# First expert layer in two halves of slots, v shift on VectorE, weight loads spread between scatters

## The chip, the cores and the metric

The kernel runs on one core of a Trainium2 chip (trn2). The metric is the device time of one execution in microseconds (us). A run is one execution, and a result below is the median of several. "Span" is the time from the first to the last instruction in the trace of one profiled execution; here time is the span plus about 2 us.

On three of the five occasions on which the kernel before was timed beside others it took 246 to 247 us, on the other two 262 to 263 us. I call these **fast chips** and **slow chip(s)**; only runs of one call share a chip. Chips 6, 1 and 12 were fast and chip 15 slow (the first call's chip is not on record). Each was timed in one call only, so a property of a chip cannot be told from a state that it was in.

## The reference, cut to what matters

```python
# q, k, v: (4, 8, 768, 64); heads 0, 2, 6 causal ("retrieval"), the other five: 4 sink keys and a window of 64
scores = q @ k.transpose(0, 1, 3, 2) / sqrt(64)          # masked per head
a = softmax(scores);  attn = a @ v
x = attn.transpose(0, 2, 1, 3).reshape(3072, 512)         # one row per token
for e in range(8):                                        # mixture of 8 experts
    mask = domain_id == e                                 # 3072 tokens, random expert each
    out[mask] = relu(x[mask] @ w1[e]) @ w2[e]             # w1: 512x1024, w2: 1024x512
```

Each expert gets about 384 tokens. The kernel gives it 448 slots (`CAP`), scatters each token's row into its slot in DRAM, and reads the slots back expert by expert.

## The kernel before, in the parts that the change touches

Attention goes batch by batch. Within a batch, short rounds of TensorE score products are mixed with older output products. The rows of batch b-1 are scattered in the middle of batch b. GpSimd issues all these scatters and all weight loads, in program order.

```python
    for b in range(B):
        ...
        vshift(b)                                   # 4 copies on GpSimd
        run_round([s_str_pair(b, 0, 0), ...], r0 + ...)
        run_round([s_str_pair(b, 1, 0), ...], r1 + t_units(b, 3))
        ...
        run_round([s_str_one(b, 2), s_sinks(b)], r2)
        if b:
            for t in range(NSO):                    # NSO = 6 blocks of 128 tokens
                scatter_x(b - 1, t)
        run_round([s_retr_pair(b, 3, 0), ...], [a_str_unit(b, 0)])
        if b + 2 < B:
            load_qk(b + 2, False); load_v(b + 2)
        if 0 < b < 3:
            load_w(wA, b - 1)                       # w1 and w2 of one expert, 2 MB
        ...
    for f in carry[0] + carry[1]:                   # last attention outputs
        f()
    for t in range(NSO):
        scatter_x(B - 1, t)
    load_w(wA, 2)
    ...
    load_x(0); load_x(1)                            # wait for every scatter; rows of 1 KB
    warm(16, "moe")                                 # junk matmuls
    x_transpose(0)
    load_w(wB, 3)
    for e in range(E):
        layer1(e)                                   # 32 matmuls of 448 columns
        if e + 1 < E: x_transpose(e + 1)            # 16 transposes, 3 VectorE copies
        if e + 2 < E: load_x(e + 2)
        layer2(e)                                   # 24 matmuls of 512 columns, scatter of the result
        if e + 4 < E: load_w(wB, e + 4)
```

`vshift` builds a copy of v in which odd 64-token blocks sit half a tile lower, so that the window of a streaming head lies in one tile.

The softmax here doesn't subtract the row's maximum and nothing guards it: scores larger than these inputs give would overflow.

## Time and profile before

| | time, median of 3 | lowest to highest | profiled execution |
|---|---|---|---|
| kernel before | 261.46 us | 261.29 to 263.63 | 245.93 us, span 244.1 us |

The profiled execution is some 16 us shorter than the timed ones.

Busy time by stretch of the trace (for each engine: busy us and number of instructions, then the granted TensorE clock as a share of full speed, the share of the DMA engines as the view gives it, which can pass 1, and GB/s), kernel before. PE is TensorE, PEld its weight loads, DVE VectorE, ACT ScalarE, POOL GpSimd, SP SyncE:

```profile
core 0: us, PE busy (x) PEld busy (x) DVE busy (x) ACT busy (x) POOL busy (x), PEclk, DMA share, GB/s
...
90.00:105.00 15.00, 11.81 (x249) 8.11 (x240) 9.70 (x25) 12.74 (x20) 8.84 (x15) 1.00 0.72 152
...
105.00:120.00 15.00, 3.87 (x28) 1.72 (x26) 1.10 (x3) 0.00 (x0) 9.69 (x16) 0.79 0.41 94
120.00:135.00 15.00, 8.89 (x47) 4.84 (x48) 1.30 (x3) 2.75 (x3) 0.00 (x0) 0.65 1.15 234
150.00:180.00 30.00, 30.00 (x178) 14.92 (x176) 8.66 (x15) 7.34 (x8) 12.63 (x21) 1.00 1.14 240
```

TensorE (PE) does 3.87 us of work in the 15 us from 105 on, and is busy without a gap from 150 to 180. The first row and the last are two stages, attention and experts; the hole is between them. What TensorE waits for there, from its list of waits (waited for: us in total, times, longest us):

```profile
PE tpx_0_2291 L767 <- DMA xe_2267<-x_slots: 16.4, 1, 16.4
```

`tpx` are the transposes of an expert's slots, `xe` the slots loaded; further below, `xT` are the transposed slots, `h` and `o` the products of the first and second layer, and `ob` the output copies. The loads can only start when the last scatter, issued 107.0 to 114.4 us, is done.

Three engines in batch 0 and later, kernel before. From GpSimd's timeline (start us, us, engine line op, [idle before <- releaser]), the shift of batch 0:

```profile
26.20 1.50 POOL L521 COPY vsh_123<-ve_145 64x1584 f16<-64x1584 f16 x1
27.74 1.28 POOL L522 COPY vsh_123<-ve_145 64x1320 f16<-64x1320 f16 x1
29.07 0.51 POOL L521 COPY vsh_123<-ve_145 64x396 f16<-64x396 f16 x1
29.64 0.46 POOL L522 COPY vsh_123<-ve_145 64x330 f16<-64x330 f16 x1
```

From TensorE's timeline, the product that waits for it:

```profile
29.63 0.21 PE L478 MATMUL avs_0_441<-vsh_123,eS_0_1_321 128*64 128x65 f16 x1 [4.70 <-POOL vsh_123 L521]
```

And from VectorE's timeline, the same small multiply with and without a GpSimd copy under way (the copy's line, from GpSimd's timeline, stands last):

```profile
86.88 0.17 DVE L224 TENSOR_TENSOR kbd<-kT_1_1731,ct 128x8 f16<-128x8 f16 x1
...
88.79 0.82 DVE L224 TENSOR_TENSOR kbd<-kT_2_1772,ct 128x8 f16<-128x8 f16 x1
...
88.09 1.50 POOL L521 COPY vsh_124<-ve_987 64x1584 f16<-64x1584 f16 x1
```

The multiply ends at 89.61 us, the copy at 89.59. The other such meeting in this trace is alike: the multiply took 0.97 us (65.74 to 66.71) and ended 0.02 us after the copy (65.19 to 66.69).

### The profile page before, as it was taken

How to read it: one execution, taken by the hardware profiler on the slowest of the kernel's cores; microseconds unless marked ns; L12 is line 12 of the kernel's file. 1: busy time of each engine (PE TensorE's matmuls, PEld its weight loads, DVE VectorE, ACT ScalarE, POOL GpSimd, SP SyncE). 2: the span in 40 equal slices, each digit the busy share in tenths (PEclk: the TensorE clock that was granted, in tenths of full speed). 3: DMA queues.
4: the chain of work that ended last, by engine and by line, in shares of the span. 5: the costliest groups of instructions: out<-in, count | busy, mean ns of one | idle time of the engine just before them, and what ended most of it. 6: DMA issues, size and time to landing. Idle time of an engine off the chain costs nothing. (4 is left out here: it accounts for less than half of the span.)

```text
span 244.1 us, 5013 instructions
## 1 busy us (share of the span) xinstructions
PE 187.0 (77%) x2077; PEld 108.3 (44%) x2077; DVE 98.0 (40%) x232; ACT 96.6 (40%) x133; POOL 109.6 (45%) x165
## 2 busy tenths in 40 slices
PE   6374269879748986880039999999999999999930
PEld 2262136756634773540024555454545454455410
DVE  0577093687995587420020313223240404141220
ACT  2157047789765798910003232141405050323200
POOL 8741956048937476538300161616154313313240
PEclk9657555799995799998557999999999999999985
DMA  6999999903999999302999999999999991203120
GB/s 121 221 212 175 196 173 201 126 34 103 169 178 200 227 256 214 104 26 103 180 242 229 220 262 197 248 245 221 276 231 278 226 266 64 82 3 121 44 83 1
DMA packets 55026, 41.26 MB, mean 169 GB/s; under 512 B 27196, under 2 KB 48596, under 8 KB 54998
## 3 DMA queue, kind: packets, MB, share of 16 engines
q0 software_dynamic: 49392, 35.67, 87.6%
q1 hardware_dynamic: 5606, 5.22, 7.9%
q8 instruction: 17, 0.28, 0.4%
q14 instruction: 11, 0.09, 0.1%
HBM read 56.62 MB, written 11.53 MB: 279 GB/s over the span
## 5 line engine op out<-in xcount | busy, mean ns | idle before, releaser
L767 PE MATMUL tpx_0_2291<-ct,xe_2267 128*128 128x128 f16 x8 | 1.0, 311 | 16.4 <-DMA xe_2267<-x_slots 16.4
L503 POOL DMA_INDIRECT x_slots<-xb_252,dest_i x6 | 6.4, 1062 | 12.1 <-ACT qT_3_868 L217 11.0
L794 ACT ACTIVATE hT_2316<-h_0_0_2317 128x896 f16<-128x896 f32 x1 | 0.9, 917 | 26.1 <-PE h_0_0_2317 L787 26.1
L801 POOL DMA_INDIRECT out_dram<-ob_2391,idx_i x1 | 1.1, 1053 | 21.3 <-DVE ob_2391 L800 21.3
L503 POOL DMA_INDIRECT x_slots<-xb_736,dest_i x6 | 6.4, 1067 | 6.1 <-DVE xb_736 L425 5.0
L767 PEld LDWEIGHTS <-xe_2267 128*128 128x128 f16 (+1 forms) x16 | 1.4, 137 | 17.1 <-DMA xe_2267<-x_slots 16.9
L503 POOL DMA_INDIRECT x_slots<-xb_1775,dest_i x6 | 5.9, 982 | 6.9 <-issue 6.9
L771 DVE COPY xT_2290<-tpx_0_2291 128x1024 f16<-128x1024 f16 x1 | 0.7, 690 | 20.2 <-PE tpx_0_2291 L767 20.2
L503 POOL DMA_INDIRECT x_slots<-xb_1286,dest_i x6 | 6.1, 1008 | 2.3 <-ACT eS_3_1926 L371 1.2
L258 PEld LDWEIGHTS <-ct 128*128 128x128 f16 x72 | 4.9, 111 | 4.8 <-issue 4.8
L787 PEld LDWEIGHTS <-w_0_990 128*128 128x128 f16 x32 | 3.4, 109 | 4.7 <-issue 2.5
L527 PEld LDWEIGHTS <-zt 128*128 128x128 f16 x26 | 2.7, 111 | 5.1 <-issue 2.0
L527 PE MATMUL warm_start<-zt 128*128 128x512 f16 x10 | 3.8, 556 | 1.3 <-DVE zt L669 1.3
L186 DVE COPY vs_sink<-vpat 128x1320 f16<-128x1320 f16 x1 | 2.2, 2232 | 6.3 <-DMA vpat<-vpat_c 6.3
L478 PEld LDWEIGHTS <-eS_0_1_321 128*64 128x64 f16 x24 | 1.9, 150 | 6.5 <-issue 6.5
L191 POOL DMA_DIRECT2D vs_sink<-in_v_dram x5 | 2.9, 577 | 4.0 <-DMA k_136<-in_k_dram 2.1
L180 POOL DMA_DIRECT2D ve_158<-in_v_dram x1 | 2.2, 2216 | 5.1 <-DMA ve_145<-in_v_dram 5.1
L801 POOL DMA_INDIRECT out_dram<-ob_3139,idx_i x1 | 1.0, 980 | 7.8 <-DVE ob_3139 L800 7.8
L787 PEld LDWEIGHTS <-w_7_2818 128*128 128x128 f16 x32 | 3.1, 98 | 3.0
L787 PEld LDWEIGHTS <-w_5_2565 128*128 128x128 f16 x32 | 3.1, 98 | 3.0
L787 PEld LDWEIGHTS <-w_1_1533 128*128 128x128 f16 x32 | 3.1, 98 | 3.0
L787 PEld LDWEIGHTS <-w_3_2312 128*128 128x128 f16 x32 | 3.1, 98 | 3.0
(887 smaller groups left out, 630.7 us busy)
## 6 DMA issues: line engine op xcount, KB each, us to landing
x_slots<-zt SPq DMA_DIRECT2D x8, 128.0 KB, 7.1
w_0_990<-in_moe_w_dram POOLq DMA_DIRECT2D x1, 1024.0 KB, 17.6
w_0_992<-in_moe_w_dram POOLq DMA_DIRECT2D x1, 1024.0 KB
w_1_1533<-in_moe_w_dram POOLq DMA_DIRECT2D x1, 1024.0 KB, 11.5
w_1_1535<-in_moe_w_dram POOLq DMA_DIRECT2D x1, 1024.0 KB
w_2_2241<-in_moe_w_dram POOLq DMA_DIRECT2D x1, 1024.0 KB, 9.1
w_2_2243<-in_moe_w_dram POOLq DMA_DIRECT2D x1, 1024.0 KB, 15.7
w_3_2312<-in_moe_w_dram POOLq DMA_DIRECT2D x1, 1024.0 KB, 21.4
```

The source lines that it names most:

```text
L180: nc.gpsimd.dma_start(out=ves[b][:, :, :, 0:D].rearrange("p h t d -> p (h t) d"), in_=v[b].rearrange("h (t p) d -> p (h t) d", p=P),)
L186: nc.vector.tensor_copy(out=vs_sink[:], in_=vpat[:].unsqueeze(1).to_broadcast([P, B, 5, VW]))
L191: nc.gpsimd.dma_start(out=vs_sink[r0 : r0 + 4, :, SIDX[h], 0:D], in_=v[:, h, 0:4, :].rearrange("b s d -> s b d"),)
L258: nc.tensor.matmul(out=dst[:, a0 : a0 + P], lhsT=ident, rhs=m_diag, start=False, stop=(n == len(diag) - 1))
L478: nc.tensor.matmul(out=pss[it][hp : hp + 64, s, 0 : D + 1], lhsT=et[:, 64 * a : 64 * a + 64], rhs=rhs[:, 0 : D + 1], start=(it == 0), stop ...
L503: ins = nc.gpsimd.indirect_dma_start(out=xs_dram, out_offset=bass.IndirectOffsetOnAxis(ap=dest_i[:, t : t + 1], axis=0), in_=xbs[b][:, it, :],
L527: nc.tensor.matmul(out=ps[:, i % 2, :], lhsT=zt[:, 0:P], rhs=zt[:], start=True, stop=True)
L767: nc.tensor.transpose(out=ps[:, j, c, 0:n], in_=xe[e][0:n, g, c * P : (c + 1) * P], identity=ident[0:n, 0:n])
L771: nc.vector.tensor_copy(out=xT[e][:, :, 0:256].rearrange("p c (j n) -> p c j n", j=2), in_=ps[:].rearrange("p j c n -> p c j n"),)
L787: nc.tensor.matmul(out=sc[:, j, 0:CAP], lhsT=w1t[:, c, ft * P : (ft + 1) * P], rhs=xT[e][:, c, :], start=(c == 0), stop=(c == 3),)
L794: nc.scalar.activation(out=hT[e][:, 2 * fp : 2 * fp + 2, :], in_=sc[:, :, 0:CAP], func=AF.Relu)
L801: ins = nc.gpsimd.indirect_dma_start(out=out, out_offset=bass.IndirectOffsetOnAxis(ap=idx_i[:, col : col + 1], axis=0), in_=ob[:], in_offs ...
```

## The change

The intent: use the hole. Slots 0 to 223 of an expert are filled by batches 0 to 2 already (the kernel checks that on the data, with a general path if it is not so), so the first layer of experts 0 to 3 can run on them while the last rows are still being scattered. Around that, the v shift leaves GpSimd, weight loads are issued one at a time, and slot rows are laid out so that a partition reads two or four neighbouring slots as one run of 2 or 4 KB. Cut to its core:

```diff
+HC = CAP // 2          # 224
+GS = CAP // 4          # 112
-            nc.gpsimd.tensor_copy(out=vshs[b][lo, ss, :, :], in_=ves[b][lo, hs, :, :])
+            nc.vector.tensor_copy(out=vshs[b][lo, ss, :, :], in_=ves[b][lo, hs, :, :])
 ...
+    def load_x(pool, e, g0, g1):
+        ...
+            in_=xs_dram[r0 : r0 + GS * n, :].rearrange("(p g) d -> p g d", p=GS)   # runs of n KB
+        for s in scatters: ...                        # waits for the scatters issued so far
+    def x_transpose(pool, e, g0, g1):
+        dst = xT[e][:, :, GS * g0 : GS * g1].rearrange("p c (m j) -> p c j m", j=n)
+            ...                                       # 8 transposes
+            nc.vector.tensor_copy(out=dst[:, :, g2 : g2 + 2, :], in_=ps[:, :, :, 0:GS])
 ...                                                  # in the loop over batches:
+        if b: scatter_all(b - 1)                      # one round earlier than before
+        if b == 2: load_w1(wA, 2, bufs=4)
+        if last:
+            for e in range(NE0): load_x(m_pool, e, 0, 2)     # first halves, 4 experts
+            load_w2(wA, 0)
 ...
+        if b == 2: load_w1(wA, 3, bufs=4)
+        if last: load_w2(wA, 1)
 ...                                                  # batch 0: streaming outputs one round later
-    for f in carry[0] + carry[1]:
+    for f in carry[0:NSO] + tx[0] + carry[NSO:] + tx[1]:     # transposes before the last output
         f()
-    for t in range(NSO): scatter_x(B - 1, t)
-    load_w(wA, 2)
+    scatter_all(B - 1)
 ...
-    load_x(0); load_x(1); warm(16, "moe"); x_transpose(0); load_w(wB, 3)
+    for e in range(NE0): load_x(m_pool, e, 2, 4)             # second halves
+    nc.gpsimd.tensor_copy(out=junk[:, 1:2], in_=xe[0, 2][0:1, 0, 0:1])   # holds what follows
+    load_w2(wB, 2, bufs=6); load_w2(wB, 3, bufs=6)
+    for e in range(NE0):
+        layer1_half(e, 0)                                    # 32 matmuls of 224 columns
+        if e + 2 < NE0: x_transpose(m_pool, e + 2, 0, 2)
+    x_transpose(m_pool, 0, 2, 4)
     for e in range(E):
-        layer1(e)
+        layer1_half(e, 1) if e < NE0 else layer1(e)
```

The order of a few small routing steps and constants changes too; the argument does not rest on them.

## The prediction

> **What bounds the kernel now.** Timeline and stretch table of the profile (span 244.1 us, TensorE busy 77%): attention runs to 105.4 us, its four batches starting at about 14.5, 46.5, 65.6 and 87.7 us. From 127.9 to 233.9 us TensorE runs the expert layers almost without a gap (30.00 of 30 us busy in 150-180), the tail is 10 us. Between them lies a hole. The last scatter of token rows is issued 107.0-114.4 us, the slot loads at 116.1, and the first lands 9.2 us later because 4 MB of weights were queued just ahead of it (waits view: TensorE waits 16.4 us for that load). Layer 1 starts at 127.9 us with 8 matmuls at half speed (3.01 against 1.68 us). So about 22 us of TensorE are lost, filled only with warm-up matmuls. A second hole is in batch 0: TensorE waits at 24.9-29.6 us for the v shift on GpSimd (copies of 1.50+1.28+0.51+0.46 us), then until 36.6 us because VectorE's routing work delays the normalization.
>
> **What the change does.**
> 1. Slots 0-223 of an expert need only batches 0-2. Their rows for experts 0-3 can be loaded after the third scatter (issued about 91.5-99 us on the old time base, some 2 us earlier than before), and four half layers run in the hole. A 448-column matmul takes 190 ns[...].
> 2. First weights are loaded during attention, one at a time, and the last two behind the second slot load: those loads (229 KB, 2 KB runs) should land in 3-5 us, not 9.
> 3. v shift goes to VectorE: I estimate 1.5 us per batch (192 fp16 copy: 0.18 us) instead of 3.8 us on GpSimd. It ends slowdowns of VectorE: a 128x8 multiply took 0.97 us instead of 0.17, a mask multiply 1.88 for two instead of 1.02, exactly while GpSimd copied[...].
> 4. Batch 0: the streaming output comes a round later, so the shift is covered: about 4 us.
>
> **On the critical path.** Batch 0: -4 us. Batches 1-3: about 0, as ScalarE and VectorE limit them. First slots land near 101-102 us, TensorE may stall 1-2 us at the transposes placed before the last attention output. Last scatter ends near 112, its slots land near 117-118. Second halves start near 119.5 us; remaining TensorE work is 104.8-12.1-1.4 = 91.3 us, ending near 211 (233.9 before). Span about 221-222; time follows by the same difference: **239.5 us, range 233 to 248**. Chances: faster 0.96, same 0.03, slower 0.01.
>
> **What would show it right.** TensorE over 85% busy from 104 to 118 us; half layers of about 3.1 us; the 16.4 us wait for the slot load replaced by waits under 3 us; batch 1 starting near 42; no VectorE 128x8 multiply near 1 us; the expert stage still 100% busy with no waits for weights.
>
> **What would make it wrong.** First slots land late (two weight loads are queued beside them), stalling TensorE before the last attention output and so delaying the last scatter; VectorE held by a shift waiting for v in batches 0-1[...]; half-clock TensorE in the half layers; 224-column matmuls bound by weight loads; out scatters waiting behind weight loads.

The sum came to 239.5 us: a span of 221 to 222 us instead of 244.1, and the time less by the same difference. The 12.1 and 1.4 us that the sum takes off stand as estimates; half of the 190 ns that a 448-column matmul takes in the profile before gives an estimated 12.2 us for the half layers (4 x 32 x 95 ns). The 3 to 5 us for a slot load are an estimate without a source; the nearest loads in that profile, 162 and 192 KB issued by SyncE, landed in 2.3 and 3.9 us.

## The result, and the profile after

| | median | lowest to highest | runs |
|---|---|---|---|
| before | 262.25 us | 261.29 to 263.63 | 4 |
| after | 239.5 us | 238.21 to 241.23 | 4 |

The ratio is 0.913 (95% interval 0.905 to 0.921). Here and below a ratio is the mean time of one kernel's fast runs over the mean time of the other's fast runs of the same rounds, so it is not quite the ratio of the medians.

The profile after is of an execution of 241.23 us, span 239.3 us. The same stretches, kernel after:

```profile
90.00:105.00 15.00, 11.68 (x233) 8.25 (x230) 9.55 (x22) 9.83 (x14) 6.46 (x13) 0.73 0.44 103
...
105.00:120.00 15.00, 11.85 (x188) 9.43 (x188) 7.18 (x18) 8.35 (x13) 2.95 (x5) 0.81 1.02 198
120.00:135.00 15.00, 11.38 (x127) 10.78 (x124) 3.46 (x3) 6.31 (x7) 7.28 (x13) 1.00 0.64 184
150.00:180.00 30.00, 29.09 (x207) 17.14 (x206) 11.94 (x13) 6.20 (x7) 15.50 (x26) 1.00 1.15 252
```

From TensorE's timeline, kernel after: the first half layers follow the last attention output (`av`) directly.

```profile
115.18 0.83 PE L447 MATMUL av<-ve,eT 128*128 128x65 f16 x21
115.84 0.56 PE L720 MATMUL tpx<-ct,xe 112*128 112x112 f16 x8
116.89 3.23 PE L808 MATMUL h<-xT,w 128*128 128x224 f16 x32 [0.49 <-DVE xT L725]
```

The hole is gone: from the end of attention to the first expert matmul there were 22.5 us (105.4 to 127.9), now there is 0.9 us (116.0 to 116.9). But attention ends 10.6 us *later* than in the profile before. That comparison crosses chips. From the list of waits of TensorE up to 118 us, kernel after:

```profile
PE avs L467 <- ACT xb L499: 9.8, 6, 3.4
```

In this trace TensorE's completion signals come up to 3.3 us after the modelled end of the last matmul that could have sent them, at 50 to 56, 77 to 83, 102 to 106 and 124 to 127 us, during or just after the issue of row scatters; the first profile before has none later than 0.3 us. So attention is probably slower for a reason that the change did not bring, or did not bring alone, and the two profiles cannot simply be subtracted. The first experiment was for that.

VectorE's groups, kernel after (busy us, mean ns of one | idle before), show one cost that the change did bring:

```profile
L725 DVE COPY xT<-tpx 128x896 f16<-128x896 f16 x16 | 25.8, 1661 | 42.1 <-PE tpx L720 36.6 <-remote 5.5
```

Before, the copies to `xT` were three per expert of 0.69, 0.42 and 0.28 us, 11.0 us in all for the same elements (group means of before_again below).

### The profile page after: what moved, and what is told of

It is laid out like the page before. It is cut to its first block, busy times and chain, and to the rows that moved or that the text cites. A ratio compares the mean times of both kernels' runs of the same rounds, so it can differ in the third digit from the quotient of the medians.

```text
span 239.3 us, 5233 instructions
## 1 busy us (share of the span) xinstructions
PE 191.1 (80%) x2190; PEld 123.1 (51%) x2190; DVE 114.6 (48%) x240; ACT 97.7 (41%) x133; POOL 97.4 (41%) x156
## 5 line engine op out<-in xcount | busy, mean ns | idle before, releaser
L842 POOL DMA_INDIRECT out_dram<-ob,idx_i x28 | 27.7, 989 | 57.6 <-DVE ob L841 52.3
L506 POOL DMA_INDIRECT x_slots<-xb,dest_i x24 | 24.3, 1013 | 56.7 <-ACT eS L349 26.8
L860 PE MATMUL o<-w,hT 128*128 128x512 f16 x192 | 43.4, 379 | 3.6 <-DVE ob L841 3.6
L725 DVE COPY xT<-tpx 128x896 f16<-128x896 f16 x16 | 25.8, 1661 | 42.1 <-PE tpx L720 36.6
L835 ACT ACTIVATE hT<-h 128x896 f16<-128x896 f32 x16 | 14.7, 917 | 41.6 <-PE h L828 41.6
L860 PEld LDWEIGHTS <-hT 128*128 128x128 f16 x192 | 18.4, 98 | 25.3 <-issue 4.7
L815 ACT ACTIVATE hT<-h 128x896 f16<-128x896 f32 x16 | 14.6, 917 | 36.9 <-PE h L808 31.6
L808 PE MATMUL h<-xT,w 128*128 128x224 f16 x256 | 26.0, 259 | 4.1 <-issue 1.8
L808 PEld LDWEIGHTS <-w 128*128 128x128 f16 x256 | 24.3, 98 | 5.7 <-issue 3.8
L828 PE MATMUL h<-xT,w 128*128 128x448 f16 x128 | 24.9, 353 | 0.0
L288 ACT ACTIVATE eT<-scr 128x896 f16<-128x896 f32 x24 | 20.7, 914 | 4.0 <-PE scr L261 2.3
L828 PEld LDWEIGHTS <-w 128*128 128x128 f16 x128 | 12.4, 98 | 12.3 <-issue 0.8
L491 DVE RECIPROCAL rcps<-avs 128x5 f32<-128x5 f32 x24 | 4.6, 191 | 22.5 <-PE avs L481 12.6
L349 ACT ACTIVATE eS<-scs 128x768 f16<-128x768 f32 x16 | 12.1, 811 | 5.7 <-PE scs L329 5.6
L210 PE MATMUL tpq<-ct,q 128*64 128x128 f16 x192 | 12.2, 287 | 2.4 <-DMA q<-in_q_dram 1.5
```

The source lines that it names most:

```text
L288: nc.scalar.activation(out=eR[b, pi][:, :, 448 * c : 448 * c + 448], in_=st["sc"][:, :, 0:448], func=AF.Exp, scale=scale)
L506: ins = nc.gpsimd.indirect_dma_start(out=xs_dram, out_offset=bass.IndirectOffsetOnAxis(ap=dest_i[:, t : t + 1], axis=0), in_=xbs[b][:, it, :],
L725: nc.vector.tensor_copy(out=dst[:, :, g2 : g2 + 2, :], in_=ps[:, :, :, 0:GS])
L808: nc.tensor.matmul(out=sc[:, i // 2, HC * (i % 2) : HC * (i % 2) + HC], lhsT=w1s[e][:, c, ft * P : (ft + 1) * P], rhs=xT[e][:, c, HC * hf ...
L815: nc.scalar.activation(out=hT[e][:, 4 * fq : 4 * fq + 4, HC * hf : HC * hf + HC].rearrange("p (j i) n -> p j i n", j=2), in_=sc[:, :, 0:CA ...
L828: nc.tensor.matmul(out=sc[:, j, 0:CAP], lhsT=w1s[e][:, c, ft * P : (ft + 1) * P], rhs=xT[e][:, c, :], start=(c == 0), stop=(c == 3),)
```

## The experiments

Twelve runs, all correct. "Before" is the kernel before.

| run | median us | before us | ratio to before | 95% interval |
|---|---|---|---|---|
| before_again | 246.26 | 246.96 | 0.996 | 0.986 to 1.006 |
| after_again | 229.23 | 246.96 | 0.928 | 0.922 to 0.935 |
| pool_shift | 236.82 | 246.96 | 0.959 | 0.950 to 0.968 |
| no_split | 248.49 | 246.96 | 1.009 | 1.001 to 1.018 |
| w2_late | 234.52 | 245.7 | 0.950 | 0.941 to 0.959 |
| tx_after | 229.91 | 245.7 | 0.935 | 0.927 to 0.942 |
| runs_1kb | 228.11 | 245.7 | 0.930 | 0.923 to 0.937 |
| combo | 228.03 | 245.7 | 0.927 | 0.920 to 0.934 |
| after_ref | 242.46 | 262.79 | 0.926 | 0.921 to 0.932 |
| w2_early | 240.24 | 262.79 | 0.917 | 0.913 to 0.921 |
| early_1kb | 237.06 | 262.79 | 0.893 | 0.885 to 0.902 |
| best_again | 228.69 | 246.67 | 0.930 | 0.926 to 0.935 |

Each block of equal "before" is one chip.

### before_again and after_again: the two kernels on one chip

No edit.

> The kernel before, unchanged, for a second profile: the profile that the prediction was read from showed a span of 244.1 us while the timed runs took 261 to 263 us, and the profile of the changed kernel showed 239.3 us beside 238 to 241 us. Theory A (the first profile of before was an unusually short execution): this profile shows a span near 259-261 us, with the extra 15 us as TensorE stalls inside attention while row scatters are being issued (updates of TensorE's semaphore over 1 us later than the modelled end of the matmul, as in the profile of after at 52, 101-106 and 122 us). Theory B (timed runs carry a fixed launch cost of 15 us for this kernel only): span again near 244 us while the time is 261.

> The changed kernel, unchanged. Ratio to before 0.91-0.92, span 236-239 us. If the stalls in attention (about 2 us at 52, 5 us at 101-106, 2 us at 122) belong to the run and not to the kernel, they lie elsewhere in this profile; if they belong to the kernel, at the same instructions.

Both theories about the offset fell: on this chip the kernel before takes 246 us, and span and time again differ by 2 us. The profile of before (244.3) equals the first one, so the first profile was not a freak; it most likely came from a chip of this kind, while the 261 us runs did not. The change gains 17.0 us here by the medians (246.26 to 229.23), where the first pair of results gave 22.7 us.

The two traces of this chip can be subtracted. First batch starts, ends and stages, read from the timelines (us):

| | batch 1 starts | batch 3 starts | attention ends | first expert matmul | TensorE ends | span |
|---|---|---|---|---|---|---|
| before_again | 46.6 | 88.2 | 105.3 | 127.6 | 234.1 | 244.3 |
| after_again | 44.1 | 86.0 | 109.3 | 109.8 | 220.2 | 230.4 |

TensorE's longest wait in before_again (95 to 140 us), and the first half layer in the timeline of after_again:

```profile
PE tpx L767 <- DMA xe<-x_slots: 16.2, 1, 16.2
...
109.83 4.36 PE L808 MATMUL h<-xT,w 128*128 128x224 f16 x32
```

So: attention +4.0, hole -21.8 (22.3 to 0.5), expert stage +3.9 (106.5 to 110.4), together -13.9 us for this pair. (The profiled execution of after_again was the slowest of its four and lies over 1.5% above the fastest, so it is listed as slow; the three others had spans of 226.6 to 227.9.) I read no late completion signals in either trace; TensorE's wait of 9.8 us for `xb` in the trace after is 1.9 and 2.8 us here. Two losses are to be explained: the end of attention and the expert stage. TensorE's waits over the whole of after_again, cut to the two kinds that answer:

```profile
PE tpx L720 <- DMA xe<-x_slots: 4.8, 1, 4.8
PE o L860 <- DVE ob L841: 3.6, 4, 0.9
...
PE h L808 <- DVE xT L725: 1.2, 1, 1.2
```

4.8 us is one wait in batch 3, for the first slots, and 3.6 us are four waits in the expert stage, for VectorE. The first half layer, behind that wait, took 4.36 us, the next one 3.23; the granted clock was 0.53 from 105 to 110 us.

### pool_shift: the v shift back on GpSimd

```diff
-            nc.vector.tensor_copy(out=vshs[b]...)
+            nc.gpsimd.tensor_copy(out=vshs[b]...)      # all four, at the new place in the program
```

> Only the v shift goes back from VectorE to GpSimd. If the move matters: VectorE's 128x8 multiply and mask multiplies slow to 1 us while GpSimd copies, batch 0 waits for the shift about 2 us longer, GpSimd issues the next loads 4 us later; 2 to 4 us slower than after (ratio to before 0.92-0.93). If it is off the critical path: within 1 us of after.

7.6 us slower than after_again by the medians, about twice what was expected. The trace says where: batch 1 starts at 48.4 us, 4.3 us later than after_again. From GpSimd's and TensorE's timelines of pool_shift:

```profile
31.63 2.34 POOL L180 DMA_DIRECT2D ve<-in_v_dram  x1
34.01 1.50 POOL L524 COPY vsh<-ve 64x1584 f16<-64x1584 f16 x1
```

```profile
37.44 0.21 PE L481 MATMUL avs<-vsh,eS 128*64 128x65 f16 x1 [11.27 <-POOL vsh L524]
```

At its new place in the program the shift stands behind 10.5 us of load issues on GpSimd (23.5 to 34.0 us), so this edit charges the shift with more than its own 3.8 us. Moving it to VectorE is worth something in its own right, but the 7.6 us are those of "GpSimd at this place", and the rest of them I did not trace. The slowdowns of VectorE that were expected came only in part: the twelve 128x8 multiplies took 0.17 us on average, one of them 0.22; the six 128x512 multiplies of the routing took 0.95 us on average instead of 0.69. The four copies took 1.67 us per batch on VectorE (3.86 on GpSimd), and in after_again the small multiply takes 0.17 us in the two stretches where the kernel before had it slow.

### no_split: everything except the split

```diff
-            for e in range(NE0):
-                load_x(m_pool, e, 0, 2)              # after the third scatter
+                                                     # moved behind the last scatter
+    for e in range(NE0): load_x(m_pool, e, 0, 2); load_x(m_pool, e, 2, 4)
+    warm(16, "moe"); then the transposes of experts 0 and 1
```

> The first half layers leave the hole: the first slot halves are loaded only after the last scatter, as are the second halves; 16 warm-up matmuls stand in the hole as before; all else as in after. If filling the hole is the main gain, as predicted (13-14 us of half layers and transposes moved into it): 11 to 15 us slower than after, about 251-254 us, ratio to before 0.96-0.97. If the gain came mostly from attention: under 6 us slower than after.

19.3 us slower than after_again, and 1.5 us slower than the kernel before of its own rounds by the medians. So without the split, everything else in the change gains nothing in the end (the split alone, without the rest, was not run), although attention ends at 100.6 us, 4.7 us sooner than in before_again. The time is lost on the way: the expert stage takes 118.3 us (118.2 to 236.5) instead of 106.5. From its waits between 95 and 145 us (11.6 us of them stand in the hole, the rest around the first half layers):

```profile
PE tpx L720 <- DMA xe<-x_slots: 16.0, 3, 11.6
```

The half layers are slower too, 5.69 us for the first and 8.89 us for the last two instead of 3.23 and 6.30, at a granted clock of 0.54 from 105 to 120 us and 0.73 from 120 to 135. So what the split gains is the filled hole and the clock behind it together.

And 100.6 us for the end of attention, beside 109.3 in after_again, says what the split costs: with no slot loads and no transposes in batch 3, that batch took 17.3 us instead of 23.3.

### w2_late: the second-layer weights behind the first slots

```diff
-            load_w2(wA, 0)                            # beside the slot loads
-            load_w2(wA, 1)
+    nc.gpsimd.tensor_copy(out=junk[:, 2:3], in_=xe[1, 0][0:1, 0, 0:1])   # before the last outputs
+    load_w2(wA, 0); load_w2(wA, 1)
```

> Edit: in the changed kernel the second-layer weights of experts 0 and 1 (1 MB each) are no longer issued beside the first slot loads in batch 3; a small GpSimd copy that reads expert 1's slots holds them back until those have landed. Theory A (these two loads stand ahead of the slot loads in the DMA engines, and the 4.8 us wait of TensorE for the first slots, with the tail of batch 3 behind it, comes from that): first slots land about 5 us earlier relative to the third scatter, the wait falls to under 1 us, the last scatter starts 4 to 5 us earlier, time 3 to 6 us under the changed kernel. Rival B (the slot loads are slow by themselves: 224 KB in row-sized pieces behind the scatter of the same rows): the wait stays near 4 to 5 us, time within 1 us of the changed kernel or longer, as the weights come later.

Half of theory A came true and the time still went the other way: 5.3 us more than after_again, by medians of two chips whose "before" agree within 1.3 us (ratio 0.950 against 0.928). TensorE's timeline of w2_late:

```profile
99.90 0.57 PE L720 MATMUL tpx<-ct,xe 112*128 112x112 f16 x8
100.31 0.82 PE L447 MATMUL av<-ve,eT 128*128 128x65 f16 x21
101.70 0.57 PE L720 MATMUL tpx<-ct,xe 112*128 112x112 f16 x8 [0.57 <-DMA xe<-x_slots]
...
122.76 0.93 PE L720 MATMUL tpx<-ct,xe 112*128 112x112 f16 x8 [7.43 <-DMA xe<-x_slots]
```

The first slots are there 4.6 us after the third scatter's last issue (95.3 to 99.9), where after_again took 9.4 (97.8 to 107.2), and the wait in front of the last attention output is gone. It came back as 7.43 us in front of the *second* slots, and the half layer behind that wait took 5.88 us instead of 3.24. The reason stands in the DMA issues between 103 and 125 us (KB each, median us from issue to landing), w2_late:

```profile
w<-in_moe_w_dram POOLq DMA_DIRECT2D x3, 1024.0 KB, 14.8
xe<-x_slots SPq DMA_DIRECT2D x4, 224.0 KB, 3.6
...
x_slots<-xb,dest_i POOLq DMA_INDIRECT x6, 11.8
```

Now the rows of the last scatter take 11.8 us to land, behind the two weights. Rows with no weights issued just ahead of them land in 2.8 us: after_again shows that from 77 to 110 us (median of eight, the third scatter's six among them; 2.4 us for its last three).

### tx_after: the slot transposes behind the last attention output

```diff
-    for f in carry[0:NSO] + tx[0] + carry[NSO:] + tx[1]:
+    for f in carry + tx[0] + tx[1]:
```

> Edit: in the changed kernel the transposes of expert 0's first slots, which TensorE meets before its last attention output and on which it waits 4.8 us for the slots, go behind that output. The last scatter then starts about 6 us earlier (near 106 us instead of 111.8). Theory A (after the hole is filled TensorE is busy without a gap until the second slots are there, so the last scatter is no longer on the critical path): only the last output's own 1.4 us moves into the wait, time 1 to 2 us under the changed kernel. Rival B (the last scatter and the second slots still bound the expert stage): time 4 to 6 us under the changed kernel.

229.91 us, ratio 0.935: no gain that these runs can tell. The premise failed as well. The last output ends at 102.1 us, 7.2 us sooner, but the last scatter starts at 110.5, only 1.3 us sooner. GpSimd's timeline of tx_after:

```profile
110.51 1.05 POOL L506 DMA_INDIRECT x_slots<-xb,dest_i  x1 [12.03 <-DMA xe<-x_slots]
```

The last scatter writes the DRAM tensor that the four slot loads read, so it waits for all four to land. In after_again that wait probably stood hidden behind the later last output. So late slot loads also held up the last scatter, by 12.0 us here, with TensorE's last output long done.

### runs_1kb: slot rows one by one, contiguous copies

```diff
-    ...rearrange("(p g) d -> p g d", p=GS)            # runs of 2 or 4 KB
+    ...rearrange("(g p) d -> p g d", p=GS)            # rows of 1 KB
-    dst = ....rearrange("p c (m j) -> p c j m", j=n)  # every n-th column
+    dst = ....rearrange("p c (j m) -> p c j m", j=n)  # contiguous columns
```

> Edit: in the changed kernel the slot rows are loaded as single 1 KB rows again (a partition takes slots 112 apart), so the copy after the transposes writes contiguous columns instead of every second or fourth one. Theory A (the copies to xT took 1.67 us on average, 16 of them 25.8 us, against 11.1 us for all of the kernel before, because they write with a stride, and VectorE then comes late to the output copies): copies near 0.6 to 0.9 us, the 3.6 us in which TensorE waits for output copies and most of the 1.2 us for xT vanish, time 3 to 5 us under the changed kernel. Rival B (the longer runs earn their keep: slot loads land 1 to 3 us later with 1 KB rows, and the first slots are on the critical path): time within 1 us of the changed kernel or longer.

The mechanism of theory A is confirmed in the trace. From VectorE's timeline of after_again, a late expert with four slots per partition and the output copies behind it:

```profile
157.39 4.14 DVE L725 COPY xT<-tpx 128x896 f16<-128x896 f16 x2 [2.77 <-PE tpx L720]
161.33 1.30 DVE L841 COPY ob<-o 128x512 f32<-128x512 f32 x2
```

and TensorE, after_again, held up by it:

```profile
157.58 3.62 PE L860 MATMUL o<-w,hT 128*128 128x512 f16 x16
162.10 1.89 PE L860 MATMUL o<-w,hT 128*128 128x512 f16 x8 [0.90 <-DVE ob L841]
```

The same copies in runs_1kb, from VectorE's timeline:

```profile
157.46 1.16 DVE L725 COPY xT<-tpx 128x896 f16<-128x896 f16 x2 [2.77 <-PE tpx L720]
```

An 896-column copy takes 0.62 us contiguous, 1.15 us into every second column, 2.07 us into every fourth. So the step to every second column costs 0.53 us a copy, and the one to every fourth another 0.92. The four waits of 0.9 us vanished, and TensorE was busy 30.00 of 30 us in both stretches from 150 to 210.

The time moved less: 228.11 against 229.23 us on another chip, ratios 0.930 and 0.928, which is the same. The expert stage took 109.4 us (106.7 to 216.1) against 110.4, because the gain was taken back inside it, at the second slots. From TensorE's timeline, runs_1kb:

```profile
122.96 0.57 PE L720 MATMUL tpx<-ct,xe 112*128 112x112 f16 x8 [2.75 <-DMA xe<-x_slots]
124.25 4.90 PE L808 MATMUL h<-xT,w 128*128 128x224 f16 x32 [0.72 <-DVE xT L725]
```

In after_again TensorE was still busy with half layers when the second slots came, and the half layer behind them took 3.24 us. Here the half layers began 3.1 us sooner, but the second slots came only 0.7 us sooner, behind a last scatter that waits for the first slot loads (14.5 us in GpSimd's list of waits), as in tx_after. The first slots still cost a wait of 2.29 us. Slot loads landed in 8.8 us (median, 95 to 125 us) against 8.2 in after_again, too little to tell whether rows of 1 KB are slower to load.

### combo: all three together

> All three edits together: second-layer weights of experts 0 and 1 behind the first slots, transposes behind the last attention output, slot rows loaded one by one. If the three are independent: span near 220 us on a chip where the changed kernel has 228 to 230, time 7 to 10 us under the changed kernel, ratio to the kernel before near 0.895. If they overlap (the slots' wait is taken away only once by the first two): 5 to 7 us under it.

228.03 us, ratio 0.927: no better than the changed kernel within the intervals. The parts do not add up: even the second expectation had 5 to 7 us, and by the medians of two chips it is 1.2. TensorE still waits 3.1 us for slots in that trace.

### after_ref, w2_early, early_1kb: the same weights earlier instead of later

```diff
+        if last:                                      # before the third scatter
+            load_w2(wA, 0); load_w2(wA, 1)
         if b: scatter_all(b - 1)
-            load_w2(wA, 0)
-            load_w2(wA, 1)
```

early_1kb has the edit of runs_1kb besides.

> The changed kernel unaltered, as the yardstick for the two runs beside it. Earlier it had 229.2 us median on one chip and 239.5 on another; here 228 to 230 is expected if the kernel before shows about 246, and 238 to 240 if it shows about 262. TensorE waits 4 to 5 us for the first slots where the trace has no late TensorE completions.

> Edit: the second-layer weights of experts 0 and 1 are issued before the third scatter (GpSimd stands idle for some 10 us there[...]) instead of behind it. Theory A (the slot loads, and through the write-after-read wait the last scatter too, stand behind these 2 MB; moved later they stand in front of the second slots, as w2_late showed, so only an earlier place frees both): first slots land 4 to 6 us after the third scatter's last issue instead of 9.4, all four loads land before the last attention output, the last scatter starts within 3 us of that output, TensorE's wait for slots falls under 1.5 us in total; time 3 to 6 us under the changed kernel beside it. Rival B (the queue has no room there either): the rows of the third scatter land up to 10 us late behind the weights, the wait for the first slots stays at 4 us or more, time within 1.5 us of the changed kernel.

> Edit: the same, and slot rows loaded one by one so that the copies to xT write contiguously. Theory: with runs_1kb the expert stage lost its 3.6 us of waits for output copies (60.0 of 60 us busy from 150 to 210), but slot waits of 5.0 us hid part of it; with the weights out of the way both gains stand: 6 to 9 us under the changed kernel beside it, ratio to the kernel before near 0.90. Rival: the slot loads in 1 KB rows are what is slow, then no better than w2_early by more than 1.5 us.

This call fell on the slow chip: before 262.79 us, the changed kernel 242.46. Here the theory held in direction: no trace of the two shows a TensorE wait for slots; the last scatter starts 1.9 us after the last output in w2_early (117.4 to 119.3); 2.2 us are gained by the medians, fewer than the 3 to 6 expected (the intervals of the ratios just touch); after_ref had no wait for slots to lose on this chip either. Where those 2.2 us lie the traces do not show, as the profiled execution of w2_early (241.89 us) is no faster than that of after_ref (240.99). Nor was the DMA queue as empty before the third scatter as hoped: after_again moved 212 GB/s from 85 to 90 us, 139 from 90 to 95 and 80 from 95 to 100. The contiguous copies give another 3.2 us. early_1kb is 5.4 us faster than the changed kernel beside it (237.06 against 242.46 us; its slowest run, 239.72, is under the other's fastest, 240.99). Of its six runs one took 232.2 us, and so four were put down as slow; the ratio of 0.893 rests on two runs, and the medians give 0.902.

I read the late completion signals of TensorE again in all three traces of this chip, at 52 to 56, 79 to 84, 100 to 107 and 120 to 128 us, and in no trace of a fast chip. I did not settle what causes them.

### best_again: the same kernel on a fast chip

> The same kernel as early_1kb, for a second timing on whatever chip it meets, because four of its six runs were put down as slow beside one very fast run, so that its ratio rested on two. If the kernel before shows about 246 us here: 222 to 226 us, ratio 0.90 to 0.92, TensorE waiting under 1.5 us for slots and the last scatter within 3 us of the last attention output. If it shows about 262 us: 235 to 238 us again, ratio 0.89 to 0.91. A time of 228 us or more beside 246 would say that the earlier weights gain nothing where TensorE completes on time.

228.69 us beside 246.67, ratio 0.930: over the 228 us named as the mark at which the earlier weights gain nothing where TensorE completes on time. The slots were late again. From the issues between 77 and 110 us, best_again:

```profile
w<-in_moe_w_dram POOLq DMA_DIRECT2D x4, 1024.0 KB, 17.8
xe<-x_slots SPq DMA_DIRECT2D x4, 224.0 KB, 3.8
x_slots<-xb,dest_i POOLq DMA_INDIRECT x7, 13.0
```

and TensorE's timeline:

```profile
107.68 0.93 PE L720 MATMUL tpx<-ct,xe 112*128 112x112 f16 x8 [5.74 <-DMA xe<-x_slots]
```

Four weights of 1 MB are now issued within 4 us (77.1 to 80.6), because the two first-layer weights wait in GpSimd's program for the second scatter. At the 200 GB/s of this stretch (80 to 100 us) 4 MB would take an estimated 21 us. The slot loads land 3.8 us after their issue, as wanted, but are issued only at 104.7 us, because the rows of the third scatter, behind the weights, take 13.0 us to land. The expert stage itself is 5.0 us shorter than in after_again (110.3 to 215.7: 105.4 us, against 110.4).

So three places for the same 2 MB gave three traffic jams: beside the slot loads (107.2 us for the first slots), behind them (the second slots 7.4 us late), ahead of them (107.7 us). Of the versions run, early_1kb beats both kernels clearly on the slow chip, and on the fast chips it is level with the changed kernel.

## Why the prediction was right or wrong

The time was predicted as 239.5 us and came out as 239.5 us. The agreement of the decimals is luck, and part of the reasoning was wrong on the way.

- **The base.** The sum was made on a profile with a span of 244.1 us and applied to timed runs of 261.46 us, "time follows by the same difference". No run shows a launch cost of 17 us: time is span plus 2 us everywhere. The offset was, most likely, a difference between chips, and the prediction came out on the scale of the slow one because the result was measured there too. On fast chips the changed kernel takes 229 us, which the stated range of 233 to 248 does not hold.
- **The hole and what fills it: right, and shown.** From 22.3 us to 0.5 us on one chip. Half layers: 3.23 us, predicted about 3.1 (32 matmuls of 224 columns measured 3.23 us, 101 ns each; half of the 190 ns for 448 columns would be 95), but 4.36 for the first one, with a granted clock of 0.53 from 105 to 110 us and 0.79 from 110 to 115; the prediction had named a low clock as a risk and not costed it. no_split shows that the gain of the change as a whole hangs on the split: without it, the rest of the change is 0.9% slower than before, within 2% and so the same.
- **Batch 0, -4 us: about right.** Batch 1 starts at 44.1 us in after_again instead of 46.6, 2.5 us sooner (predicted: near 42). The other fast-chip traces with the same batch 0 have it between 41.1 and 44.2 us, and the first trace after at 42.9.
- **v shift, 1.5 us per batch on VectorE: right** (1.67), and the small multiply is at 0.17 us. What the GpSimd place costs was measured only together with its place in GpSimd's queue.
- **"First slots land near 101-102 us" and "loads should land in 3-5 us": the step that failed.** Third scatter at 90.3 to 97.8 us, as predicted (about 91.5 to 99), but first slots at 107.2. The loads took 8.7 us in the window after the third scatter, because the 2 MB of w2 for experts 0 and 1 were issued with them. The wait is 4.8 us instead of 1 to 2, and so over the "under 3 us" for slot waits. The prediction named this as a way to be wrong and still budgeted too little. w2_late shows the cause (4.6 us from last issue to first slots without these loads) and also that the bytes cannot be moved for nothing. What follows was late with it: the last scatter ended at 119.3 us (predicted near 112), its first slots were there at 123.7 (117 to 118), and the second halves began at 125.8 (119.5). That is 6.3 of the 9.2 us by which TensorE ended late in after_again.
- **"The expert stage still 100% busy": wrong.** 28.19 of 30 us in after_again; 3.6 us lost to output copies and 1.2 us to `xT`, both behind strided copies that the prediction did not cost at all. runs_1kb takes away all of the first and 0.5 us of the second. The stage took 110.4 us in after_again and 110.9 in tx_after, a fast execution with the same copies; the sum in the prediction (12.1 + 91.3 us) made it 103.4.
- **The end of TensorE work**, predicted 211 us, was 220.2 in after_again, whose profile is of a slow execution (218.7 in tx_after, whose is not); the difference by the medians was 17.0 us instead of 22. The mis-sized terms are the first-slot wait, with what it delays, and the copies.
- **"TensorE over 85% busy from 104 to 118 us": wrong.** 10.79 of 14 us in after_again (77%), the slot wait standing in it.

What stays open: why the slow chip is 16 us slower on the kernel before (there is no profile of it there), what the late TensorE completions on that chip are, and so why the change gains 20 to 23 us there and 17 us elsewhere. The profiles of the slow chip show no wait for slots, which fits the difference, but this was not tested. A rival stands beside the late completions: the granted clock of the kernel before was 0.80 to 0.82 in the fast runs on chip 15 and 0.85 to 0.87 on the fast chips. Whether a lower clock slows attention there, or stalls lower the clock, no run separates.

## What to carry to other kernels

When a hole is filled with work whose data must come in beside other loads, cost the queue and not the load: ask which bytes stand ahead in the DMA engines at that moment, and which write waits for which read of the same tensor, since moving 2 MB of weights later or earlier only moved the jam on the fast chips here. Count a wait of TensorE for more than itself: the half layer behind it took 3.51 us (best_again) to 5.88 us (w2_late) instead of 3.23. Before choosing a memory layout for longer DMA runs, cost the on-chip copy that has to undo it; here 1.15 to 2.07 us instead of 0.62. And check that the profile and the timed runs come from the same kind of chip before adding a predicted difference to a measured time.
